# GeGLU feed-forward on one core: contraction chunks of neighbouring features, x transposed in two half rows and by transposing transfers

## The chip, the cores and the metric

The kernel runs on one core of a Trainium2 chip. The metric is device microseconds of one execution. Before the change the median of three runs is 299.9 us (299.17 to 300.43). The execution that was profiled took 299.69 us; its profile spans 298.4 us. TensorE's granted clock in the profile is 1.00.

## What is computed

```python
B, S, D, F = 32, 32, 1024, 3584            # x is (32, 32, 1024), all bf16
def reference(x, w_gate, w_up, w_down):
    return (_gelu(x @ w_gate) * (x @ w_up)) @ w_down    # _gelu: tanh approximation
```

With N = 32 x 32 = 1024 tokens: x is [1024, 1024], the gate and up weights are [1024, 3584], the down weights [3584, 1024], the output [1024, 1024]. The sum over D is cut into 8 chunks of 128 features (`dk`), F into 28 chunks of 128 rows of the hidden layer (`m`).

## The kernel before, in words

**Two large stages on TensorE.** In the first (L388) the weights are the stationary operand (128 features x 128 hidden rows), and transposed x (`xT`, features on the partitions, tokens along the free axis) moves. For each hidden chunk `m` and a block of tokens there are 8 gate matmuls and 8 up matmuls, which add up over `dk` in PSUM. ACT applies gelu to the gate sum (L446), DVE multiplies with the up sum and writes `hT` (L486). The second stage (L425) multiplies `hT` with the down weights; ACT and DVE by turns copy the sums out (L452, L492), and SP stores them (L344). A tuple of hidden chunk and token block is a *part*. Parts 0 to 7 are hidden chunks 0 to 7 with tokens 0 to 255; parts 8 to 15 the same hidden chunks with tokens 256 to 511; from part 16 on tokens come in blocks of 512.

**Which features are a chunk.** The program may choose which 128 of the 1024 features form a chunk, as long as weights and x agree. In the kernel before, partition p of chunk k holds feature 8p + k: `"(p k) f -> p k f"` for both weights (L211, L212). A chunk of x is then every eighth element of a row.

**How x gets transposed.** x lies in DRAM with tokens in rows; `xT` wants features on the partitions. Three ways are used:

- Tokens 0 to 255 are loaded into `xa` in two pieces of 128 tokens with whole rows of 2 KB: `xa` side 0 from SP, side 1 from ACT (L293). Chunks 0 to 4 are transposed on TensorE by a matmul with the identity (`turn_xa`, L349 to L360), ten matmuls into PSUM banks 3, 4 and 5 (`XA_PS`: bank 3 holds chunk 0, bank 4 chunks 1 and 2, bank 5 chunks 3 and 4). ACT copies each bank to `xT` (L439), three copies.
- Chunks 5 to 7 of those tokens are transposed by DVE in 32 x 32 blocks, sixteen instructions (L462).
- Tokens 256 to 1023 are loaded to `xs` in twelve pieces (`load_x`, L284, half from SP, half from ACT), laid out so that twenty DVE transposes (L477) fill `xT`. They are mixed by hand between the first products on DVE (`dve_order`, L186 to L194).

**Order of the work.** Every engine runs its instructions in program order, and waits are on semaphores. TensorE's order is the list `steps` (L156 to L183). It begins with seven warm-up matmuls of ones (L402), then the ten transposes, token side 0 before token side 1 (first chunks 0 to 2, then 3 and 4). Then come, with chunk 0, gate matmuls of parts 0, 1, 2, 3, 7, 6, 4, up matmuls of parts 0 to 3, the gate matmul of part 5, and up matmuls of 7, 6, 4, 5. A part whose PSUM bank was used by a transpose (3, 4, 5) has to wait for ACT's copy of that bank (L377 to L379). `together` then runs chunks 1 to 5 through all eight parts, and the parts are finished in two halves. Parts 8 to 11 follow with tokens 256 to 383 for chunks 0 to 3, tokens 384 to 511 for the same chunks, and the rest in 256 columns. All other parts go `one_by_one`.

**Queues.** SP issues its half of `xa`, then the weights of hidden chunks 0 to 7, one chunk `dk` at a time, gate and up in turn, 256 KB each (L289; the last chunk in two halves), then waits for up chunk 5 and issues its x pieces. After those have landed (`gate_w`, L308) SP loads the first small gate weight group and POOL the first small up group (L278). Later groups and the down weights wait for TensorE. ACT issues its half of `xa` and, after its three copies, its x pieces.

Of the kernel before, what the change touches and what calls it, by code (L numbers as in the profile page):

```python
# [5 lines left out]
P = 128  # L6
# [3 lines left out]
ALU = mybir.AluOpType  # L10
# [74 lines left out]
def bass_standalone__geglu_ffn__sampling_kernel(  # L85
# [40 lines left out]
    XC = N // 32  # L126
    XE = D // 4
    XA, XB, XC2 = (0, 256), (256, 512), (512, 1024)
    XB1, XB2 = (256, 384), (384, 512)
    XPIECES = [XB1, XB2, XC2]  # L130
# [5 lines left out]
    for t0, t1 in (XA, XB):  # L136
        for m in range(NBIG):
            parts.append((m, t0, t1, (m, 0, 256), (m, 256, 512)))
# [19 lines left out]
    def together(ps_, k0, k1, tok=None):  # L158
        for dk in range(k0, k1):
            for key in ("G", "U"):  # L160
                for p in ps_:
                    steps.append((p, key, dk, tok))

    def one_by_one(ps_, k0):
        for p in ps_:
            for key in ("G", "U"):
                for dk in range(k0, DK):
                    steps.append((p, key, dk, None))
# [12 lines left out]
    together(range(8, 12), 4, 6)  # L181
    one_by_one(range(8, 12), 6)
    one_by_one(range(12, NPART), 0)  # L183


    dve_order = []  # L186
    mix = ("E0 E1 E2 A0 E3 A1 A2 A3 B0 B1 B2 B3 E4 D4 D5 E5 D6 D7 E6 E7 "
           "C0 E8 C1 E9 C2 E10 E11 C3 C4 E12 C5 E13 C6 C7 E14 E15")
    for w in mix.split():
        if w[0] == "E":  # L190
            dve_order.append(("E", int(w[1:])))
        else:
            dve_order.append(("T", int(w[1:])) + {"A": XB1, "B": XB2, "C": XC2, "D": XB}[w[0]])
    dve_order += [("E", p) for p in range(NSHORT, NPART)]  # L194
# [15 lines left out]
    x_r = xf.rearrange("(c i) (a e) -> a i c e", i=32, a=4)  # L210
    wg_r = w_gate.rearrange("(p k) f -> p k f", k=DK)  # L211
    wu_r = w_up.rearrange("(p k) f -> p k f", k=DK)  # L212
# [7 lines left out]
    Q_X = {(q, s): _Clock(f"x{i}{s}", 16) for i, q in enumerate(XPIECES) for s in range(2)}  # L220
# [7 lines left out]
    all_clocks = [C_PE, C_ACT, C_DVE, C_POOL, *Q_XA, *Q_X.values(), *Q_W0.values(), *Q_W7.values(), *Q_WG, *Q_WU,  # L228
# [4 lines left out]
    with ExitStack() as es:  # L233
# [6 lines left out]
        assert 8 * N == XC * XE  # L240
        xs = hT[:, FM - 8:FM, :].rearrange("p a (b e) -> p (a b) e", e=XE)
# [39 lines left out]
        def load_x(ew, eng, q, side):  # L281
            c0, c1 = q[0] // 32, q[1] // 32
            for a in (2 * side, 2 * side + 1):
                v = ew.do(lambda: eng.dma_start(  # L284
                    xs[32 * a:32 * (a + 1), c0:c1, :], x_r[a, :, c0:c1, :]), clock=Q_X[(q, side)])
            ctx.set(("x", q, side), v)
# [5 lines left out]
        def early_loads(ew, eng, side):  # L292
            ctx.set(("xa", side), ew.do(lambda: eng.dma_start(  # L293
                xa[:, side, :], xa_r[:, side, :]), clock=Q_XA[side]))
            yield
            if side == 0:
                for k in range(DK - 1):
                    for w in ("wg", "wu"):
                        load_w0(ew, eng, w, k, 0, NBIG * P, Q_W0[(w, k)])
                for h in range(2):  # L300
                    for w in ("wg", "wu"):
                        load_w0(ew, eng, w, DK - 1, h * GSZ * P, (h + 1) * GSZ * P,
                                Q_W7[w] if h else Q_W0[(w, DK - 1)])
            ew.wait(Q_W0[("wu", 5)], ctx.get(("wu0", 5, 0)))
# [25 lines left out]
        def prog_sp(eng):  # L330
            sp = _Eng(ctx, eng, None)
            for _ in early_loads(sp, eng, 0):
                pass
# [13 lines left out]
            sp.wait(Q_OUT, last)  # L347

        def turn_xa(pe, eng, b, dk):  # L349
            pe.wait(Q_XA[b], ctx.get(("xa", b)))  # L350
            j = next(j for j, (_, k0, k1) in enumerate(XA_PS) if k0 <= dk < k1)
            bank, k0, k1 = XA_PS[j]
            o = 256 * (dk - k0) + P * b
            last = dk == k1 - 1 and b == 1
            v = pe.do(lambda: eng.matmul(  # L355
                ps[:, bank, o:o + P],
                xa[:, b, :].rearrange("p (j k) -> p j k", k=DK)[:, :, dk],
                ident[:, :], start=(dk == k0 and b == 0), stop=last), mark=last)
# [38 lines left out]
        WARM = [512] * 7  # L397
# [35 lines left out]
        def prog_act(eng):  # L433
            act = _Eng(ctx, eng, C_ACT)
            act.do(lambda: eng.activation(warm[:, 0:1], const0, ACTF.Gelu_apprx_tanh))
            for _ in early_loads(act, eng, 1):
                for j, (bank, k0, k1) in enumerate(XA_PS):
                    act.wait(C_PE, ctx.get(("XP", j)))
                    ctx.set(("XA", j), act.do(lambda: eng.activation(  # L439
                        xT[:, k0:k1, XA[0]:XA[1]],  # L440
                        ps[:, bank, 0:256 * (k1 - k0)].rearrange("p (k t) -> p k t", t=256), ACTF.Copy)))
# [13 lines left out]
        def prog_dve(eng):  # L455
            dve = _Eng(ctx, eng, C_DVE)

            for b in range(2):
                dve.wait(Q_XA[b], ctx.get(("xa", b)))
            for q in range(4):  # L460
                for a in range(4):
# [4 lines left out]
                            "p b (j k) -> p k b j", k=DK)[:, XA_DVE[0]:XA_DVE[1], :, 32 * a:32 * (a + 1)]))  # L466
            ctx.set("XD", v)
            for what in dve_order:
                if what[0] == "T":
                    dk, q = what[1], what[2:]  # L470
                    landed = [r for r in XPIECES if q[0] <= r[0] < q[1]]
                    for r in landed:
                        for s in range(2):
                            dve.wait(Q_X[(r, s)], ctx.get(("x", r, s)))
                    src = xs[:, q[0] // 32:q[1] // 32, :].rearrange(
                        "p c (j k) -> p c j k", k=DK)[:, :, :, dk]
                    v = dve.do(lambda: eng.transpose(  # L477
                        xT[:, dk, q[0]:q[1]].rearrange("p (c i) -> p c i", i=32), src))
                    for r in landed:
                        ctx.set(("T", dk, r), v)  # L480
                else:
                    i = what[1]
                    m, t0, t1, _gs, (ub, u0, u1) = parts[i]
                    dve.wait(C_ACT, ctx.get(("A", i)))
                    dve.wait(C_PE, ctx.get(("U", i)))
                    ctx.set(("D", i), dve.do(lambda: eng.tensor_tensor(  # L486
                        hT[:, m, t0:t1], t_bufs[i % NTB][:, 0:t1 - t0], ps[:, ub, u0:u1], ALU.mult)))
# [56 lines left out]
```

## Time and profile before

| what | us |
|---|---|
| median of the runs (3) | 299.9 (299.17 to 300.43) |
| the profiled execution | 299.69 |
| span of its profile | 298.4 |
| TensorE matmuls busy (PE) | 294.2 |
| DVE busy | 64.3 |
| ACT busy | 42.2 |
| first weights of stage one at TensorE | 5.18 |
| first matmul of parts 8 to 11 | 19.48 |
| first weights of the 512-column parts | 33.54 |
| start of stage two in the chain | 199.57 |

Times in the profile are microseconds from the start of its span. PE is TensorE's matmuls and PEld its weight loads, which run beside matmuls; SPq, ACTq and POOL lines with DMA in them are the issues of transfers. Each line of the timeline gives start, length, engine, line of the program, operation, output and inputs, the number of instructions merged into the line, and in brackets how long the engine was idle before it and what released it. Matmuls are pipelined, so a matmul's length is longer than the distance from one to the next; distances are read from the starts of the weight loads.

### The profile page before, as it was taken

To read this page: it belongs to the slowest core of one execution; us is meant where nothing else is said; L and a number is where in the kernel's file an instruction comes from. 1 tells how busy PE (TensorE), PEld (TensorE's weight loads), DVE (VectorE), ACT (ScalarE), POOL (GpSimd) and SP (SyncE) were. 2 spreads that over 40 slices of the span, in tenths; PEclk is the share of its full clock that TensorE was granted. 3 is DMA by queue.
4 is the path that set the end of the run, shared out by engine and by line. 5 is a ranking of instruction groups with operands and counts; after the bars stand their busy time and mean duration, and the time that the engine had idled before them with its cause. 6 is when DMAs were issued, how large, how long until landed. Compare 5 with 4: busy or idle time off the path is not lost.

```text
span 298.4 us, 3487 instructions
## 1 busy us (share of the span) xinstructions
PE 294.2 (99%) x1525; PEld 149.3 (50%) x1549; DVE 64.3 (22%) x108; ACT 42.2 (14%) x78; POOL 7.9 (3%) x14
## 2 busy tenths in 40 slices
PE   8999999999999999999999999999999999999997
PEld 5899644444444444444444444444444444444446
DVE  4669722111122111122111112110000000000000
ACT  3032211121111121111112111110000000000000
POOL 1001001020001002001000000000000000000000
PEclk9999999999999999999999999999999999999999
DMA  7997104856008301942104000000000100010001
GB/s 255 386 205 234 51 2 125 296 181 244 0 0 295 129 0 27 371 167 93 49 0 141 0 2 0 0 0 20 18 18 18 37 18 18 20 35 18 18 20 35
DMA packets 18094, 26.43 MB, mean 89 GB/s; under 512 B 1056, under 2 KB 11936, under 8 KB 18080
## 3 DMA queue, kind: packets, MB, share of 16 engines
q1 hardware_dynamic: 14128, 16.78, 17.3%
q0 software_dynamic: 2176, 8.39, 7.9%
q10 hardware_dynamic: 1776, 1.05, 1.4%
q8 instruction: 12, 0.20, 0.3%
q14 instruction: 2, 0.02, 0.0%
HBM read 24.12 MB, written 2.10 MB: 88 GB/s over the span
## 4 chain that ended last, share of the span: by engine, by line
PE 99%; issue 0%; ACT 0%
PE ps L388 65%; PE ps L425 32%; PE ps L402 1%; PE ps L355 0%; ACT xT L452 0%
## 5 line engine op out<-in xcount | busy, mean ns | idle before, releaser
L425 PE MATMUL ps<-wd,hT 128*128 128x512 bf16 (+1 forms) x468 | 96.5, 366 | 0.4
L388 PE MATMUL ps<-xT,wgbig 128*128 128x512 bf16 (+2 forms) x394 | 79.6, 337 | 0.3
L388 PE MATMUL ps<-xT,wubig 128*128 128x512 bf16 (+2 forms) x395 | 79.5, 336 | 0.3
L425 PEld LDWEIGHTS ps<-wd,hT 128*128 128x128 bf16 x476 | 46.6, 98 | 50.4
L486 DVE TENSOR_TENSOR hT<-tb,ps 128x512 bf16<-128x512 f32 (+1 forms) x64 | 38.9, 615 | 136.6 <-PE ps L388 136.6
L446 ACT ACTIVATE tb<-ps 128x512 f32<-128x512 f32 (+1 forms) x64 | 34.2, 544 | 158.3 <-PE ps L388 155.4
L388 PEld LDWEIGHTS ps<-xT,wgbig 128*128 128x128 bf16 x400 | 38.3, 98 | 31.7 <-DMA wgbig<-in_w_gate_dram 0.2
L388 PEld LDWEIGHTS ps<-xT,wubig 128*128 128x128 bf16 x400 | 38.1, 98 | 31.4
L388 PE MATMUL ps<-xT,wgsmall 128*128 128x512 bf16 x126 | 30.1, 379 | 0.1
L388 PE MATMUL ps<-xT,wusmall 128*128 128x512 bf16 x125 | 29.8, 379 | 0.2
L492 DVE CAST xT<-ps 128x512 bf16<-128x512 f32 (+1 forms) x8 | 5.3, 658 | 88.1 <-PE ps L425 88.1
L388 PEld LDWEIGHTS ps<-xT,wgsmall 128*128 128x128 bf16 x128 | 12.5, 98 | 15.1
L388 PEld LDWEIGHTS ps<-xT,wusmall 128*128 128x128 bf16 x128 | 12.5, 98 | 15.1
L452 ACT ACTIVATE xT<-ps 128x512 bf16<-128x512 f32 (+1 forms) x9 | 5.2, 573 | 93.1 <-PE ps L425 93.1
L477 DVE STREAM_TRANSPOSE xT<-hT 128x128 bf16<-128x128 bf16 (+2 forms) x20 | 13.4, 705 | 0.0
L462 DVE STREAM_TRANSPOSE xT<-hT 32x192 bf16<-32x192 bf16 x16 | 8.2, 514 | 4.7 <-DMA hT<-in_x_dram 4.2
L278 POOL DMA_DIRECT2D wubig<-in_w_up_dram x3 | 2.7, 884 | 62.9 <-PE ps L388 62.9
L402 PE MATMUL ps<-const-bfloat16-1.0 128*128 128x512 bf16 x7 | 3.1, 627 | 0.8 <-PEq L529 0.8
L278 POOL DMA_DIRECT2D wusmall<-in_w_up_dram x2 | 2.0, 993 | 47.9 <-PE ps L388 26.0
L272 POOL DMA_DIRECT2D wd<-in_w_down_dram x3 | 2.3, 766 | 19.1 <-PE ps L388 19.1
L402 PEld LDWEIGHTS ps<-const-bfloat16-1.0 128*128 128x128 bf16 x7 | 0.9, 139 | 2.1 <-issue 2.1
L439 ACT ACTIVATE xT<-ps 128x512 bf16<-128x512 f32 (+1 forms) x3 | 1.4, 527 | 2.4 <-PE ps L355 2.4
(10 smaller groups left out, 4.9 us busy)
## 6 DMA issues: line engine op xcount, KB each, us to landing
wd<-in_w_down_dram SPq DMA_DIRECT2D x4, 1024.0 KB, 11.3
wgbig<-in_w_gate_dram SPq DMA_DIRECT2D x3, 1024.0 KB, 5.8
wubig<-in_w_up_dram POOLq DMA_DIRECT2D x3, 1024.0 KB, 9.6
wd<-in_w_down_dram POOLq DMA_DIRECT2D x3, 1024.0 KB, 11.3
wgsmall<-in_w_gate_dram SPq DMA_DIRECT2D x2, 1024.0 KB, 5.9
wusmall<-in_w_up_dram POOLq DMA_DIRECT2D x2, 1024.0 KB, 9.7
out_dram<-xT SPq DMA_DIRECT2D x15, 128.0 KB, 1.7
wgbig<-in_w_gate_dram SPq DMA_DIRECT2D x7, 256.0 KB, 5.3
```

The lines of the kernel that those rows point to most:

```text
L272: ew.do(lambda: eng.dma_start(wd[:, a:b, :], wd_r[:, a:b, :]), clock=clock)
L278: ctx.set((w, j), ew.do(lambda: eng.dma_start(wbuf(w, buf)[:, :, 0:gsz * P], w_r[w][:, :, c0 * P:(c0 + gsz) * P]), clock=q))
L388: v = pe.do(lambda: eng.matmul(ps[:, bank, f0:f1], wbuf(w, buf)[:, dk, slot * P:(slot + 1) * P], xT[:, dk, t0:t1], start=first, stop=last ...
L402: pe.do(lambda: eng.matmul(ps[:, 0, 0:n], ones_w, ones_x[:, 0:n], start=True, stop=True), mark=False)
L425: v = pe.do(lambda: eng.matmul(ps[:, b, 0:ncols], hT[:, m, tc * P:(tc + 1) * P], wd[:, m, col0:col0 + ncols], start=(m == 0), stop=(m == F ...
L439: ctx.set(("XA", j), act.do(lambda: eng.activation(xT[:, k0:k1, XA[0]:XA[1]], ps[:, bank, 0:256 * (k1 - k0)].rearrange("p (k t) -> p k t", ...
L446: ctx.set(("A", i), act.do(lambda: eng.activation(t_bufs[i % NTB][:, 0:t1 - t0], ps[:, gb, g0:g1], ACTF.Gelu_apprx_tanh)))
L452: ctx.set(("E", ji), act.do(lambda: eng.activation(osb[:, tc, col0:col0 + ncols], ps[:, b, 0:ncols], ACTF.Copy)))
L462: v = dve.do(lambda: eng.transpose(xT[32 * a:32 * (a + 1), XA_DVE[0]:XA_DVE[1], XA[0]:XA[1]].rearrange("p k (b t) -> p k b t", t=P)[:, :, ...
L477: v = dve.do(lambda: eng.transpose(xT[:, dk, q[0]:q[1]].rearrange("p (c i) -> p c i", i=32), src))
L486: ctx.set(("D", i), dve.do(lambda: eng.tensor_tensor(hT[:, m, t0:t1], t_bufs[i % NTB][:, 0:t1 - t0], ps[:, ub, u0:u1], ALU.mult)))
L492: ctx.set(("E", ji), dve.do(lambda: eng.tensor_copy(osb[:, tc, col0:col0 + ncols], ps[:, b, 0:ncols])))
```

## The change

Chunk k now holds the neighbouring features 128k to 128k + 127, for weights and x. x's first 256 tokens are still loaded into `xa`, but in two halves of the row: piece 0 has features 0 to 511 of both token sides, piece 1 features 512 to 1023, in runs of 1 KB. Both are issued by SP, with the first gate weights between them. The matmul transposes read 128 neighbouring elements instead of every eighth; a transpose waits for the piece that has its chunk. Six of them (chunks 0 to 2, the two token sides in turn) come first, the four for chunks 3 and 4 only after the seven first gate matmuls. One warm-up matmul is left out. DVE's sixteen transposes for chunks 5 to 7 stay, read neighbouring elements and wait for piece 1 alone.

Tokens 256 to 1023 are no longer loaded to `xs` and transposed by DVE. SP issues six transposing transfers from x in DRAM straight into `xT`: two for tokens 256 to 511 (chunks 0 to 3 and 4 to 7), four for tokens 512 to 1023 (two chunks each), 256 KB each, after up chunk 6 has landed. TensorE waits for the transfer that brings a chunk, and parts 8 to 11 are no longer cut into two halves of tokens. `dve_order`, `load_x`, `x_r` and `xs` are gone, and with them ACT's issues of loads. The first small weight groups now wait for the last of the six transfers.

```diff
+    XTOK = {"B": (256, 512), "C": (512, 1024)}
+    XT = [("B", 0, 4), ("B", 4, 8), ("C", 0, 2), ("C", 2, 4), ("C", 4, 6), ("C", 6, 8)]
...
-    for k0, k1 in ((0, 3), (3, XA_DVE[0])):
-        for b in range(2):
-            steps += [("X", b, dk) for dk in range(k0, k1)]
-    for key, ps_ in (("G", (0, 1, 2, 3, 7, 6, 4)), ("U", (0, 1, 2, 3)), ("G", (5,)), ("U", (7, 6, 4, 5))):
-        steps += [(p, key, 0, None) for p in ps_]
+    steps += [("X", b, dk) for dk in range(0, 3) for b in range(2)]
+    steps += [(p, "G", 0) for p in (0, 1, 2, 3, 7, 6, 4)]
+    steps += [("X", b, dk) for dk in range(3, XA_DVE[0]) for b in range(2)]
+    steps += [(p, "U", 0) for p in (0, 1, 2, 3)] + [(5, "G", 0)] + [(p, "U", 0) for p in (7, 6, 4, 5)]
     together(range(0, 8), 1, 6)
...
-    together(range(8, 12), 0, 4, XB1)
-    together(range(8, 12), 0, 4, XB2)
-    together(range(8, 12), 4, 6)
-    one_by_one(range(8, 12), 6)
+    together(range(8, 12), 0, 4)
+    one_by_one(range(8, 12), 4)
...
-    wg_r = w_gate.rearrange("(p k) f -> p k f", k=DK)
-    wu_r = w_up.rearrange("(p k) f -> p k f", k=DK)
+    wg_r = w_gate.rearrange("(k p) f -> p k f", p=P)
+    wu_r = w_up.rearrange("(k p) f -> p k f", p=P)
...
+        def load_xa(ew, eng, h):
+            ctx.set(("xa", h), ew.do(lambda: eng.dma_start(
+                xa[:, :, 512 * h:512 * (h + 1)], xa_r[:, 0:2, 512 * h:512 * (h + 1)]), clock=Q_XA[h]))
+
+        def early_loads(ew, eng):
+            load_xa(ew, eng, 0)
+            for k in range(DK - 1):
+                for w in ("wg", "wu"):
+                    load_w0(ew, eng, w, k, 0, NBIG * P, Q_W0[(w, k)])
+                    if (w, k) == ("wg", 0):
+                        load_xa(ew, eng, 1)
...
+            ew.wait(Q_W0[("wu", 6)], ctx.get(("wu0", 6, 0)))
+            for q in XT:
+                (t0, t1), k0, k1 = XTOK[q[0]], q[1], q[2]
+                ctx.set(("xt", q), ew.do(lambda: eng.dma_start_transpose(
+                    xT[:, k0:k1, t0:t1], xf[t0:t1, k0 * P:k1 * P]), clock=Q_XT[q]))
...
-            pe.wait(Q_XA[b], ctx.get(("xa", b)))
+            pe.wait(Q_XA[dk // 4], ctx.get(("xa", dk // 4)))
...
-                xa[:, b, :].rearrange("p (j k) -> p j k", k=DK)[:, :, dk],
+                xa[:, b, dk * P:(dk + 1) * P],
...
-            for q in XPIECES:
-                if q[0] < t1 and t0 < q[1]:
-                    pe.wait(C_DVE, ctx.get(("T", dk, q)))
+            for q in XT:
+                if (t0, t1) == XTOK[q[0]] and q[1] <= dk < q[2]:
+                    pe.wait(Q_XT[q], ctx.get(("xt", q)))
...
-        WARM = [512] * 7
+        WARM = [512] * 6
...
-            for b in range(2):
-                dve.wait(Q_XA[b], ctx.get(("xa", b)))
+            dve.wait(Q_XA[1], ctx.get(("xa", 1)))
...
-                            "p b (j k) -> p k b j", k=DK)[:, XA_DVE[0]:XA_DVE[1], :, 32 * a:32 * (a + 1)]))
+                            "p b (k a i) -> p a k b i", a=4, i=32)[:, a, XA_DVE[0]:XA_DVE[1], :, :]))
```

More of the change, by code (lines that the diff above doesn't have):

```diff
@@ L120, in bass_standalone__geglu_ffn__sampling_kernel @@
     wd_gate_chunk = [min(FM - 1, 3 + 3 * k) for k in range(len(wd_groups))]
[L126 to L130, printed above, removed]
+    XA = (0, 256)
+    XTOK = {"B": (256, 512), "C": (512, 1024)}
+    XT = [("B", 0, 4), ("B", 4, 8), ("C", 0, 2), ("C", 2, 4), ("C", 4, 6), ("C", 6, 8)]
     XA_PS = [(3, 0, 1), (4, 1, 3), (5, 3, 5)]
@@ L135, in bass_standalone__geglu_ffn__sampling_kernel @@
     parts = []
-    for t0, t1 in (XA, XB):
+    for t0, t1 in (XA, XTOK["B"]):
         for m in range(NBIG):
@@ L156, in bass_standalone__geglu_ffn__sampling_kernel, with together @@
     steps = []
-    def together(ps_, k0, k1, tok=None):
+    def together(ps_, k0, k1):
         for dk in range(k0, k1):
@@ L161, in together @@
                 for p in ps_:
-                    steps.append((p, key, dk, tok))
+                    steps.append((p, key, dk))
     def one_by_one(ps_, k0):
@@ L167, in one_by_one @@
                 for dk in range(k0, DK):
-                    steps.append((p, key, dk, None))
-    for k0, k1 in ((0, 3), (3, XA_DVE[0])):
-        for b in range(2):
-            steps += [("X", b, dk) for dk in range(k0, k1)]
-    for key, ps_ in (("G", (0, 1, 2, 3, 7, 6, 4)), ("U", (0, 1, 2, 3)), ("G", (5,)), ("U", (7, 6, 4, 5))):
-        steps += [(p, key, 0, None) for p in ps_]
+                    steps.append((p, key, dk))
+    steps += [("X", b, dk) for dk in range(0, 3) for b in range(2)]
+    steps += [(p, "G", 0) for p in (0, 1, 2, 3, 7, 6, 4)]
+    steps += [("X", b, dk) for dk in range(3, XA_DVE[0]) for b in range(2)]
+    steps += [(p, "U", 0) for p in (0, 1, 2, 3)] + [(5, "G", 0)] + [(p, "U", 0) for p in (7, 6, 4, 5)]
     together(range(0, 8), 1, 6)
@@ L178, in bass_standalone__geglu_ffn__sampling_kernel @@
         one_by_one(half, 7)
-    together(range(8, 12), 0, 4, XB1)
-    together(range(8, 12), 0, 4, XB2)
-    together(range(8, 12), 4, 6)
-    one_by_one(range(8, 12), 6)
+    together(range(8, 12), 0, 4)
+    one_by_one(range(8, 12), 4)
     one_by_one(range(12, NPART), 0)
[L186 to L194, printed above, removed]
     jobs = []
@@ L209, in bass_standalone__geglu_ffn__sampling_kernel @@
     xa_r = xf.rearrange("(b p) d -> p b d", p=P)
-    x_r = xf.rearrange("(c i) (a e) -> a i c e", i=32, a=4)
-    wg_r = w_gate.rearrange("(p k) f -> p k f", k=DK)
-    wu_r = w_up.rearrange("(p k) f -> p k f", k=DK)
+    wg_r = w_gate.rearrange("(k p) f -> p k f", p=P)
+    wu_r = w_up.rearrange("(k p) f -> p k f", p=P)
     wd_r = w_down.rearrange("(m p) d -> p m d", p=P)
@@ L219, in bass_standalone__geglu_ffn__sampling_kernel @@
     Q_XA = [_Clock(f"xa{b}", 16) for b in range(2)]
-    Q_X = {(q, s): _Clock(f"x{i}{s}", 16) for i, q in enumerate(XPIECES) for s in range(2)}
+    Q_XT = {q: _Clock(f"xt{i}", 16) for i, q in enumerate(XT)}
     Q_W0 = {(w, k): _Clock(f"{w}0k{k}", 16) for k in range(DK) for w in ("wg", "wu")}
@@ L227, in bass_standalone__geglu_ffn__sampling_kernel @@
     Q_OUT = _Clock("out", 16)
-    all_clocks = [C_PE, C_ACT, C_DVE, C_POOL, *Q_XA, *Q_X.values(), *Q_W0.values(), *Q_W7.values(), *Q_WG, *Q_WU,
+    all_clocks = [C_PE, C_ACT, C_DVE, C_POOL, *Q_XA, *Q_XT.values(), *Q_W0.values(), *Q_W7.values(), *Q_WG, *Q_WU,
                   Q_WD_SP, Q_WD_POOL, Q_OUT]
@@ L239, in bass_standalone__geglu_ffn__sampling_kernel @@
         wd = sb("wd", [P, FM, D], BF16)
-        assert 8 * N == XC * XE
-        xs = hT[:, FM - 8:FM, :].rearrange("p a (b e) -> p (a b) e", e=XE)
         xa = hT[:, FM - 10:FM - 8, :]
@@ L279, in load_w @@
                 wbuf(w, buf)[:, :, 0:gsz * P], w_r[w][:, :, c0 * P:(c0 + gsz) * P]), clock=q))
[L281 to L286, printed above, removed]
         def load_w0(ew, eng, w, k, f0, f1, q):
@@ L290, in load_w0 @@
                 big[w][:, k, f0:f1], w_r[w][:, k, f0:f1]), clock=q))
[L292 to L304, printed above, removed]
-            for q in XPIECES:
-                load_x(ew, eng, q, side)
+        def load_xa(ew, eng, h):
[8 more added lines that the diff above has]
+                        load_xa(ew, eng, 1)
+            for h in range(2):
+                for w in ("wg", "wu"):
+                    load_w0(ew, eng, w, DK - 1, h * GSZ * P, (h + 1) * GSZ * P,
+                            Q_W7[w] if h else Q_W0[(w, DK - 1)])
+            ew.wait(Q_W0[("wu", 6)], ctx.get(("wu0", 6, 0)))
[3 more added lines that the diff above has]
+                    xT[:, k0:k1, t0:t1], xf[t0:t1, k0 * P:k1 * P]), clock=Q_XT[q]))
         def gate_w(ew, j):
             if war[j] is None:
-                for s in range(2):
-                    ew.wait(Q_X[(XC2, s)], ctx.get(("x", XC2, s)))
+                ew.wait(Q_XT[XT[-1]], ctx.get(("xt", XT[-1])))
                 return -1
@@ L331, in prog_sp @@
             sp = _Eng(ctx, eng, None)
-            for _ in early_loads(sp, eng, 0):
-                pass
+            early_loads(sp, eng)
             wd_mine = [k for k in range(len(wd_groups)) if k % 2 == 0]
@@ L360, in turn_xa, with part_step @@
                 ctx.set(("XP", j), v)
-        def part_step(pe, eng, opened, i, key, dk, tok):
+        def part_step(pe, eng, opened, i, key, dk):
             m, t0, t1, gs, us = parts[i]
             w, (bank, f0, f1) = ("wg", gs) if key == "G" else ("wu", us)
-            if tok is not None:
-                f0, f1 = f0 + tok[0] - t0, f0 + tok[1] - t0
-                t0, t1 = tok
             buf, slot, j = slot_of[m]
@@ L381, in part_step @@
                 pe.wait(C_DVE, ctx.get("XD"))
-            for q in XPIECES:
-                if q[0] < t1 and t0 < q[1]:
-                    pe.wait(C_DVE, ctx.get(("T", dk, q)))
+            for q in XT:
+                if (t0, t1) == XTOK[q[0]] and q[1] <= dk < q[2]:
+                    pe.wait(Q_XT[q], ctx.get(("xt", q)))
             first = (i, bank) not in opened
@@ L435, in prog_act @@
             act.do(lambda: eng.activation(warm[:, 0:1], const0, ACTF.Gelu_apprx_tanh))
[L436 to L441, printed above, removed]
+            for j, (bank, k0, k1) in enumerate(XA_PS):
+                act.wait(C_PE, ctx.get(("XP", j)))
+                ctx.set(("XA", j), act.do(lambda: eng.activation(
+                    xT[:, k0:k1, XA[0]:XA[1]],
+                    ps[:, bank, 0:256 * (k1 - k0)].rearrange("p (k t) -> p k t", t=256), ACTF.Copy)))
             for i, (m, t0, t1, (gb, g0, g1), us) in enumerate(parts):
@@ L465, in prog_dve @@
                         xa[32 * q:32 * (q + 1), :, :].rearrange(
-                            "p b (j k) -> p k b j", k=DK)[:, XA_DVE[0]:XA_DVE[1], :, 32 * a:32 * (a + 1)]))
+                            "p b (k a i) -> p a k b i", a=4, i=32)[:, a, XA_DVE[0]:XA_DVE[1], :, :]))
             ctx.set("XD", v)
[L468 to L487, printed above, removed]
+            for i, (m, t0, t1, _gs, (ub, u0, u1)) in enumerate(parts):
+                dve.wait(C_ACT, ctx.get(("A", i)))
+                dve.wait(C_PE, ctx.get(("U", i)))
+                ctx.set(("D", i), dve.do(lambda: eng.tensor_tensor(
+                    hT[:, m, t0:t1], t_bufs[i % NTB][:, 0:t1 - t0], ps[:, ub, u0:u1], ALU.mult)))
             for ji, (tc, col0, ncols, b) in enumerate(jobs):
```

## Prediction

> **What bounds the kernel now.** First the page: the span, the engine shares, the clock, the chain of what ended last.
>
> ```profile
> span 298.4 us, 3487 instructions
> PE 294.2 (99%) x1525; PEld 149.3 (50%) x1549; DVE 64.3 (22%) x108; ACT 42.2 (14%) x78; POOL 7.9 (3%) x14
> PEclk9999999999999999999999999999999999999999
> ...
> PE 99%; issue 0%; ACT 0%
> PE ps L388 65%; PE ps L425 32%; PE ps L402 1%; PE ps L355 0%; ACT xT L452 0%
> ```
>
> TensorE is the chain: 99% of it is matmuls, and DVE, ACT and the DMAs appear nowhere. In the chain in order of time the steady stretch repeats pieces of 10.74 + 0.05 us, that is 50 matmuls of 512 columns, 0.2158 us each. The change leaves those alone. It can move the time only where TensorE waits, where it runs slowly, or by making it wait. So I read the first 36 us as a timeline of TensorE's matmuls (PE) and weight loads (PEld) and of ACT.
>
> ```profile
> 0.77 3.15 PE L402 MATMUL ps<-const-bfloat16-1.0 128*128 128x512 bf16 x7 [0.77 <-PEq L529]
> 3.96 1.03 PEld L355 LDWEIGHTS ps<-ident,hT 128*128 128x128 bf16 x10 [0.96 <-issue]
> 4.65 1.36 ACT L439 ACTIVATE xT<-ps 128x256 bf16<-128x256 f32 x3 [2.43 <-PE ps L355]
> 5.18 1.08 PEld L388 LDWEIGHTS ps<-xT,wgbig 128*128 128x128 bf16 x7 [0.18 <-DMA wgbig<-in_w_gate_dram]
> 6.28 0.43 PEld L388 LDWEIGHTS ps<-xT,wubig 128*128 128x128 bf16 x4
> 6.71 0.10 PEld L388 LDWEIGHTS ps<-xT,wgbig 128*128 128x128 bf16 x1
> 6.82 0.42 PEld L388 LDWEIGHTS ps<-xT,wubig 128*128 128x128 bf16 x4
> 7.26 0.86 PEld L388 LDWEIGHTS ps<-xT,wgbig 128*128 128x128 bf16 x8
> ```
>
> Columns: start, length, engine, line. Seven warm-up matmuls, ten transposes of x by matmul, three copies of them by ACT, the first weights at 5.18, chunk 1 at 7.26; from there on no gap. The granted clock reads 1.00 throughout, but the pace tells more: warm-up weight loads are 0.425 us apart, the first 256-column ones after 5.18 about 0.21, those after 6.1 only 0.109. So **TensorE runs at half pace until about 6.1 us**.
>
> **The change, part by part.**
>
> *1. The front.* One warm-up matmul goes: the six end at 0.77 + 6 x 0.427 = 3.33 instead of 3.76. The transposes start when the first x piece lands. By the windows of one microsecond the DMAs had moved 0.31 MB by 3.0 and 0.67 MB by 4.0; the old pieces, 0.52 MB together, were complete near 3.6 and TensorE started at 3.96. The new first piece is 0.26 MB with nothing beside it, complete near 2.9. I take a start at 3.5 (bounds: 3.35, end of the warm-up; 4.0, as now).
>
> Six transposes come first, and the chunk 0 copy needs only two of them. ACT now starts 0.37 after the last transpose's weight load that it needs (4.28 to 4.65), takes 0.38, and the first weights follow 0.15 later. New: 3.5 + 0.105 + 0.37 + 0.38 + 0.15 = 4.5. The first gate weights are no obstacle: they are complete once 0.52 MB instead of 0.79 MB has moved (near 3.6 instead of 4.3; the load of up chunk 5, complete near 11.9, released SP at 12.71, a lag of 0.8), so about 4.4. The start is 0.7 earlier, but at half pace.
>
> Now the order bites. Seven gate matmuls at 0.213 end at 6.0. Only then come the four transposes of chunks 3 and 4, 0.25 at mixed pace: the last starts near 6.15. ACT's copy of them starts 0.3 later and takes 0.60 (its 512-column form), plus 0.15: part 5 may start at **7.2**. TensorE has only four up matmuls to put before it (0.44, to 6.7), then stands for 0.5 us, because it runs in order. Five matmuls follow (0.55), and chunk 1 starts at 7.74 where it now starts at 7.26: **+0.48**. In the kernel before that copy was done at 6.01, before part 5 at 6.71. Bounds: -0.02 if the copy is hidden after all (4.5 + 1.5 + 0.25 + 0.44 + 0.55 = 7.24), +0.9 if x starts at 4.0 as now.
>
> The second x piece now stands between the first weights on SP's queue; ACT's own issue (0.38) goes. Bytes up to the first up weights are unchanged (1.05 MB, near 5.1, landed 5.9), and they are wanted at 6.25. The next weight issues on SP are 0.47 later, but the DMAs are the limit there (318 to 408 GB/s; four issues in 1.9 us would be 550). Nothing for this. If it slips by 0.5 it disappears in the wait for part 5.
>
> *2. The DVE part of the first tokens (chunks 5 to 7).* Same sixteen transposes, now with neighbouring source elements. They took 8.69 us from 4.24. The second x piece lands near 5.1; at the old 0.51 each they end at 13.7, and chunk 5 is wanted at 7.74 + 4 x 1.745 = 14.7. Cover 1.0 us; at less than 0.51 each, more. If the cover is gone, what exceeds it is paid in full. Taken: nothing.
>
> *3. Weights by neighbouring rows.* Same number of 2 KB and 1 KB rows, at another pitch in DRAM. Early loads: chunk 1's weights are complete near 5.9, landed near 6.7, wanted at 7.74. Later groups are issued tens of microseconds ahead (a 1 MB load lands in 5.8 to 9.7). Taken: nothing; no row excludes a few per cent of rate either way, which this cover holds.
>
> *4. Tokens 256 to 511, no halves.* 64 matmuls of 128 columns ran from 19.48 to 23.11, that is 3.63. As 32 of 256 columns they take 32 x 0.109 = 3.49. **-0.14.**
>
> *5. DVE loses 20 transposes (13.4 us).* DVE was not in the chain; its products come earlier, and no matmul waited for one. The one wait shown for a DVE transpose, 0.17 of a weight load at 35.00, is hidden: matmuls go on at 0.216. Nothing.
>
> *6. The transposing transfers.* Six of 256 KB, on SP, after the last full up chunk but one. The 4.7 MB of early loads are unchanged, and chunk 6 completes 0.52 MB after chunk 5 at 366 to 383 GB/s: issue at 12.71 + 1.4 = 14.1. The trace has no such transfer. The nearest rows are the twelve x loads that they replace, as many bytes in runs of 512 B:
>
> ```profile
> L284 SPq DMA_DIRECT2D hT<-in_x_dram x6: 332/432/1630, 12.7 to 15.0; - x6
> L284 ACTq DMA_DIRECT2D hT<-in_x_dram x6: 368/453/1579, 12.7 to 15.0; - x6
> ...
> DMA to landing us min/median/max: 3.4/5.3/7.9
> ```
>
> Wanted: chunks 0 to 3 of tokens 256 to 511 at 19.48 + 0.48 = 19.96; chunks 4 to 7 at 23.45; tokens 512 up from 33.9 on, the last pair at 35.2. The first of the six, at the lowest to median landing, comes at 17.5 to 19.4: in time. All twelve old loads had landed by 22.9, 10.2 after issue: by that the six are in at 24.3, 11 us early. **Nothing**, if they overlap as the old ones did. Ends: no gain below nothing, since TensorE does not wait there now; at the longest landing, 7.9, the first comes at 22.0 and costs 2.0 (302.3); serial transfers are a rival below. Behind them on SP and POOL waits only the first small weight group (issued at 23.0 and 23.6 now), which is not wanted before 61, so 30 us of delay would be hidden.
>
> The Trainium skill ("DMA: Bandwidth & Descriptors", "Latency and other measured facts") gives 261 GB/s for a transposing transfer with a non-contiguous middle; by that, as an estimate, all six move in 6 us and the sum stays. The same skill ("VectorE: DVE Perf Modes", "The three transpose paths") gives 1309 ns for one 128x128 block by DMA; if blocks came one by one, an estimate of 10.5 us for each transfer and about 342 in all. No row here shows which holds.
>
> **Sum.** +0.48 - 0.14 = +0.34. The profiled execution took 299.69 (span 298.4 and 1.29 around it), 0.2 below the median 299.9. It becomes 300.03; against the median, 300.24: **300.2**. A difference under 0.5%, 1.5 us, is about what a measurement of this kernel cannot tell from no change.
>
> **Rivals.**
>
> *A, the wait in front is hidden.* Half pace ends before 6.0, or the last copy overlaps more. Chunk 1 at 7.24, sum -0.16: **299.7**. For it: only the order of one copy makes the 0.48. Against: the copy's 0.60 and the four matmuls' 0.44 are both rows.
>
> *B, half pace lasts longer.* Full pace came 5.3 us after the first matmul. The new front has holes: about 0.2 before the transposes, 0.3 before the first weights. If these restart the count at 4.5, full pace comes at 9.8. Up to chunk 1: 4.5 + 1.5 + 0.43, copy to 7.45, five matmuls at 0.213, so 8.5; then 1.3 us at half pace cost 0.65. Shift 1.9, less 0.14: **301.7**. For it: longer holes than now (0.2 and 0.15). Against: full pace came in spite of those. The Trainium skill ("TensorE: Matmul & The Clock Gate", "Part 1") says the clock is released after one busy window of some 3.4 us that runs freely; by it, as an estimate, a window missed costs 1.7.
>
> *C, slower: transposing transfers come one after another.* This is the case for the other side of no change. Place: the first matmuls of tokens 256 to 511 and of tokens 512 up. With t for each, the last pair lands at 14.1 + 6t and is wanted at 35.2: it decides from t = 3.5 on. At the median landing 5.3: the fourth chunk waits 1.25 (24.7 against 23.45), the last two pairs 4.6 and 4.9, together 10.7: **310.9**. At 7.9, 2.0 + 4.4 + 4.9 + 7.5 + 7.5 = 26.3: 326.5. For it: no row shows this kind of transfer. Against: 256 KB loads overlap on this queue (eighteen within 13 us), and 21 us of cover.
>
> *D, the change does not do what it says* (the first weights do not come earlier): within the bounds of part 1, 300.6.
>
> **Chances.** Forecast 0.60 with D in it, A 0.11, B 0.11, C 0.18 (of which up to 302.3: 0.03). Faster by over 0.5%: 0.02, a front much faster than A. Same: 0.70. Slower: 0.28, from B and C and a little of the forecast's edge. Range: forecast and A with the runs' scatter (299.2 to 300.4 around 299.9) start at 299.0; B and the late first transfer end at 302.4; outside is most of C.
>
> **What would show it.** Step 1: first gate weight load at 4.5, an idle gap of 0.5 before part 5's first gate matmul with ACT's last L439 copy as releaser, chunk 1 at 7.7. B: 256-column weight loads still 0.21 apart after 7. Step 4: 256-column matmuls 0.109 apart from 20.0. Step 6: landing under 3.5 us in effect, and no wait of PEld for xT from x in DRAM; such a wait would make the prediction wrong by its length. A span below 297 would contradict the reading that TensorE's own work bounds it.

## The result and the profile after

The changed kernel takes **300.27 us** (median of 22 runs, 299.68 to 301.99); the kernel before, measured beside it, 299.5 (22 runs, 299.17 to 300.43). The ratio is 1.0022, with a 95% interval of 1.0013 to 1.0031: slower by 0.2%, less than the 0.5% that the prediction set as its bound for "same". The forecast was 300.2. That the two agree so closely is partly luck: the prediction added +0.34 to a median of three runs (299.9) which 22 runs put at 299.5. The move was +0.77, more than twice the sum, and most of the difference lies in one term of step 1.

The page after, span, engines and chain:

```profile
span 299.1 us, 3414 instructions
PE 295.5 (99%) x1516; PEld 148.7 (50%) x1516; DVE 50.4 (17%) x88; ACT 42.4 (14%) x78; POOL 7.8 (3%) x14
...
PE 97%; DMA 2%; SPq 0%; ACT 0%; issue 0%
PE ps L362 65%; PE ps L399 32%; DMA wubig<-in_w_up_dram 2%; SPq L267 0%; SPq L263 0%; ACT xT L425 0%
```

A DMA is in the chain now, with 2% of the span: the load of up weights. Where it stands is told by the timeline of the front (L332 the transposes by matmul, L412 ACT's copies, L362 the gate and up matmuls):

```profile
3.72 0.56 PEld L332 LDWEIGHTS ps<-ident,hT 128*128 128x128 bf16 x6 [1.15 <-issue]
4.66 1.20 PEld L362 LDWEIGHTS ps<-xT,wgbig 128*128 128x128 bf16 x7 [0.38 <-DMA wgbig<-in_w_gate_dram]
5.92 0.58 PEld L332 LDWEIGHTS ps<-ident,hT 128*128 128x128 bf16 x4
6.80 0.60 ACT L412 ACTIVATE xT<-ps 128x512 bf16<-128x512 f32 x1 [1.61 <-PE ps L332]
7.17 0.33 PEld L362 LDWEIGHTS ps<-xT,wubig 128*128 128x128 bf16 x4 [0.67 <-DMA wubig<-in_w_up_dram]
7.17 0.61 PE L362 MATMUL ps<-xT,wubig 128*128 128x256 bf16 x4 [0.41 <-DMA wubig<-in_w_up_dram]
7.51 0.10 PEld L362 LDWEIGHTS ps<-xT,wgbig 128*128 128x128 bf16 x1
8.06 0.86 PEld L362 LDWEIGHTS ps<-xT,wgbig 128*128 128x128 bf16 x8
```

The first gate weights start at 4.66 instead of 5.18. But the first up weights land only at 7.13 by the chain, and TensorE waits for them until 7.17. ACT's copy of chunks 3 and 4 ends at 7.40; part 5, behind four up matmuls, loads at 7.51 without a further wait. So two ends nearly meet there. A third stands right behind them: by the landings that the trace records, the gate weights of chunk 1 landed at 8.00, 0.06 before they were used. Chunk 1 starts at 8.06 instead of 7.26. From there the two kernels are compared by distances between the same weight loads:

| stretch | before, us | after, us | difference |
|---|---|---|---|
| start of span to chunk 1 | 7.26 | 8.06 | +0.80 |
| chunk 1 to parts 8 to 11 | 12.22 | 12.23 | +0.01 |
| parts 8 to 15 | 14.06 | 13.97 | -0.09 |
| 512-column parts, to stage two | 166.03 | 166.03 | 0.00 |
| stage two to the end | 98.83 | 98.81 | -0.02 |

The sum, +0.7, is the difference of the spans (299.1 to 298.4). The transposing transfers cost nothing; the front is the whole loss.

Why are the up weights late? Windows of one microsecond, last column GB/s moved by the DMAs; first the kernel before, then the changed one:

```profile
4.00:5.00 1.00, 1.00 (x10) 1.00 (x10) 0.73 (x2) 0.35 (x2) 0.00 (x0) 1.00 1.12 354
5.00:6.00 1.00, 1.00 (x7) 0.57 (x5) 0.94 (x3) 1.00 (x3) 0.00 (x0) 1.00 0.92 318
```

```profile
4.00:5.00 1.00, 0.86 (x8) 0.56 (x6) 0.00 (x0) 0.80 (x2) 0.00 (x0) 1.00 1.18 269
5.00:6.00 1.00, 1.00 (x7) 0.69 (x6) 0.68 (x2) 0.19 (x1) 0.00 (x0) 1.00 0.84 250
```

By 6.0 us 1.13 MB have moved instead of 1.34. From 8 to 10 us the rates differ little (399 and 408 GB/s before, 391 and 401 after). The mean rate is only about half of the delay: the 1.05 MB up to the first up weights were reached near 5.7 instead of 5.1. The rest is in the last parts of the transfer. Each of these loads lands in sixteen parts, and the trace records the time of each. The parts of the first up weights landed between 5.20 and 5.82 in the kernel before and between 5.37 and 7.13 in the changed one, half of them by 6.06; TensorE needs all sixteen.

The transposing transfers of the changed kernel, the row that the prediction did not have:

```profile
L284 SPq DMA_TRANSPOSE xT<-in_x_dram x6: 1299/1302/1758, 15.4 to 22.6; - x6
...
DMA to landing us min/median/max: 3.2/3.7/4.1
```

SP spends 1.30 us on the issue of each (1.76 on the first, 0.43 on a plain load), so from the second on one starts about every 1.35 us, 194 GB/s of 256 KB pieces, and each lands about 3.7 after its issue.

### The profile page after: what moved, and what is told of

It reads as the page before. It is cut to its first block, busy times and chain, and to the rows that moved or that the text cites. A ratio compares the mean times of both kernels' runs of the same rounds, so it can differ in the third digit from the quotient of the medians.

```text
span 299.1 us, 3414 instructions
## 1 busy us (share of the span) xinstructions
PE 295.5 (99%) x1516; PEld 148.7 (50%) x1516; DVE 50.4 (17%) x88; ACT 42.4 (14%) x78; POOL 7.8 (3%) x14
## 4 chain that ended last, share of the span: by engine, by line
PE 97%; DMA 2%; SPq 0%; ACT 0%; issue 0%
PE ps L362 65%; PE ps L399 32%; DMA wubig<-in_w_up_dram 2%; SPq L267 0%; SPq L263 0%; ACT xT L425 0%
## 5 line engine op out<-in xcount | busy, mean ns | idle before, releaser
L362 PE MATMUL ps<-xT,wgbig 128*128 128x512 bf16 (+1 forms) x384 | 79.5, 346 | 0.1
L362 PE MATMUL ps<-xT,wubig 128*128 128x512 bf16 (+1 forms) x384 | 78.7, 344 | 0.4 <-DMA wubig<-in_w_up_dram 0.4
L362 PEld LDWEIGHTS ps<-xT,wgbig 128*128 128x128 bf16 x384 | 37.8, 99 | 32.1 <-DMA wgbig<-in_w_gate_dram 0.4
L362 PEld LDWEIGHTS ps<-xT,wubig 128*128 128x128 bf16 x384 | 37.5, 98 | 32.3 <-DMA wubig<-in_w_up_dram 0.7
L362 PE MATMUL ps<-xT,wusmall 128*128 128x512 bf16 x128 | 30.2, 379 | 0.0
L362 PE MATMUL ps<-xT,wgsmall 128*128 128x512 bf16 x128 | 30.2, 379 | 0.0
L362 PEld LDWEIGHTS ps<-xT,wusmall 128*128 128x128 bf16 x128 | 12.5, 98 | 15.1
L362 PEld LDWEIGHTS ps<-xT,wgsmall 128*128 128x128 bf16 x128 | 12.5, 98 | 15.1
L434 DVE STREAM_TRANSPOSE xT<-hT 32x192 bf16<-32x192 bf16 x16 | 5.9, 370 | 5.8 <-DMA hT<-in_x_dram 5.3
L412 ACT ACTIVATE xT<-ps 128x512 bf16<-128x512 f32 (+1 forms) x3 | 1.6, 526 | 3.6 <-PE ps L332 3.6
L332 PEld LDWEIGHTS ps<-ident,hT 128*128 128x128 bf16 x10 | 1.1, 141 | 1.3 <-issue 1.1
L332 PE MATMUL ps<-ident,hT 128*128 128x128 bf16 x10 | 1.4, 307 | 0.3 <-DMA hT<-in_x_dram 0.3
```

Of the source, the lines that this page charges most:

```text
L332: v = pe.do(lambda: eng.matmul(ps[:, bank, o:o + P], xa[:, b, dk * P:(dk + 1) * P], ident[:, :], start=(dk == k0 and b == 0), stop=last), ...
L362: v = pe.do(lambda: eng.matmul(ps[:, bank, f0:f1], wbuf(w, buf)[:, dk, slot * P:(slot + 1) * P], xT[:, dk, t0:t1], start=first, stop=last ...
L412: ctx.set(("XA", j), act.do(lambda: eng.activation(xT[:, k0:k1, XA[0]:XA[1]], ps[:, bank, 0:256 * (k1 - k0)].rearrange("p (k t) -> p k t", ...
L434: v = dve.do(lambda: eng.transpose(xT[32 * a:32 * (a + 1), XA_DVE[0]:XA_DVE[1], XA[0]:XA[1]].rearrange("p k (b t) -> p k b t", t=P)[:, :, ...
```

## The experiments

The theory after the result: two waits of nearly one length, for the first up weights and for ACT's copy of chunks 3 and 4, hold chunk 1; behind it nothing is lost. The rivals: one of the two alone; the rows of weights or the transposing transfers; the warm-up. The third wait, for the gate weights of chunk 1, was not in it. Medians are over 4 to 12 executions; each ratio is to the kernel before, run together with them. The last column is 260 for the changed kernel and 336 for the kernel before.

| run | median, us | ratio to before (95%) | early DMA rate, 4 to 6 us, GB/s |
|---|---|---|---|
| up weights before x's second piece | 300.95 | 1.0055 (1.0037 to 1.0074) | 241 |
| part 5 last | 300.35 | 1.0026 (1.0012 to 1.0040) | 218 |
| both | 300.13 | 1.0021 (1.0011 to 1.0030) | 306 |
| old front | 299.71 | 1.0005 (0.9994 to 1.0016) | 314 |
| x's second piece on ACT | 301.10 | 1.0036 (1.0019 to 1.0052) | 379 |
| the same, part 5 last | 301.32 | 1.0052 (1.0040 to 1.0064) | 365 |
| the same, all transposes first | 301.12 | 1.0044 (1.0028 to 1.0060) | 386 |
| whole rows, second side on SP | 302.27 | 1.0087 (1.0071 to 1.0103) | 286 |
| old front, six warm-ups | 299.65 | 0.9996 (0.9986 to 1.0007) | 361 |
| all transposes first, eight warm-ups | 299.74 | 1.0004 (0.9994 to 1.0014) | 320 |
| changed kernel, seven warm-ups | 300.47 | 1.0026 (1.0016 to 1.0036) | 247 |
| late transposing transfers | 301.52 | 1.0063 (1.0047 to 1.0078) | 235 |

**1. Up weights first.** In `early_loads`:

```diff
-                    if (w, k) == ("wg", 0):
+                    if (w, k) == ("wu", 0):
                         load_xa(ew, eng, 1)
```

> The changed kernel with one edit: the first up weights are issued before x's second half rows. In the changed kernel the first up matmul starts at 7.17, when these weights land, and chunk 1 at 8.06; ACT's copy of chunks 3 and 4 ends at 7.40. Theory 'two waits of one length' (copy and up weights each hold chunk 1 near 8.05): up matmuls start 0.5 to 0.8 earlier, then part 5 waits for the copy, chunk 1 at 8.0 to 8.1, time 300.3, no change. Theory 'up weights alone': chunk 1 at 7.4 to 7.6, time 299.7. Theory 'copy alone' (as in the prediction): no change, 300.3.

A miss in the time: it got slower. x's second piece, now third behind the weights, landed only at 7.0 and the transposes of chunk 4 waited for it; the copy then held part 5, as these lines say:

```profile
7.03 0.12 PEld L332 LDWEIGHTS ps<-ident,hT 128*128 128x128 bf16 x2 [0.85 <-DMA hT<-in_x_dram]
8.00 0.10 PEld L362 LDWEIGHTS ps<-xT,wgbig 128*128 128x128 bf16 x1 [0.53 <-ACT xT L412]
```

So TensorE can stand for this copy. But the copy was late here because x's piece was, not because of the order of steps that the prediction described, and the edit moved one load forward and another back. This run does not decide between the theories.

**2. Part 5 last.** In `steps`:

```diff
-    steps += [(p, "U", 0) for p in (0, 1, 2, 3)] + [(5, "G", 0)] + [(p, "U", 0) for p in (7, 6, 4, 5)]
+    steps += [(p, "U", 0) for p in (0, 1, 2, 3, 7, 6, 4)] + [(5, "G", 0), (5, "U", 0)]
```

> The changed kernel with one edit: both chunk 0 matmuls of part 5 come last, so that seven up matmuls (0.76 us) instead of four (0.44) stand between the late transposes and the one that needs ACT's copy. Theory 'two waits of one length': up matmuls still start at 7.17, nine matmuls of 0.109 follow, chunk 1 at 8.05 to 8.15, time 300.3, no change. Theory 'copy alone': chunk 1 at 7.6 to 7.7, time 299.8 to 299.9. Theory 'up weights alone': no change, 300.3.

No change, and the up matmuls start at 7.16, chunk 1 at 8.05. "Copy alone" falls. "Up weights alone" forecast the same as "two waits" and stays.

**3. Both edits.**

> The changed kernel with both edits: up weights before x's second half rows, and part 5 last. Theory 'two waits of one length': up matmuls start at 6.4 to 6.6, the copy (7.4) holds part 5 until 7.5, chunk 1 at 7.7, time 299.9 (0.35 less than the changed kernel). Theory 'up weights alone': the same as the first edit by itself. Theory 'copy alone': the same as the second edit by itself.

Chunk 1 at 7.70, as forecast by two waits. Part of that is not the edit: full pace came at about 5.2 in this execution, earlier than in the changed kernel's profile. The time, 300.13, is lower than the changed kernel's by less than the interval, so this run says little on its own; its lines show x's second piece late again (6.6) and a last wait of 0.20 for the copy.

**4. The old front.** `load_xa` and the order of transposes as before:

```diff
-                xa[:, :, 512 * h:512 * (h + 1)], xa_r[:, 0:2, 512 * h:512 * (h + 1)]), clock=Q_XA[h]))
+                xa[:, h, :], xa_r[:, h, :]), clock=Q_XA[h]))
...
+            load_xa(act, eng, 1)
...
-        WARM = [512] * 6
+        WARM = [512] * 7
```

> The changed kernel with the front of the kernel before: x's first tokens in two pieces of whole rows from SP and ACT, all ten transposes ahead of the first weights in the old order, seven warm-up matmuls. Rows of weights, transposing transfers and undivided parts 8 to 11 stay as changed. Theory 'the front is the whole loss': chunk 1 at 7.2 to 7.3 as before, parts 8 to 11 shorter by 0.09, time 299.4 against 299.5 of the kernel before. Rival 'transfers or rows cost something': it stays above 299.8, with a wait behind chunk 1 or slower early loads.

The median lies between the two forecasts, and the interval of its ratio includes 1, no change. The trace decides: chunk 1 starts at 6.96, parts 8 to 11 at 19.10, 512-column parts at 33.07, stage two at 199.10.

```profile
5.06 0.67 PEld L361 LDWEIGHTS ps<-xT,wgbig 128*128 128x128 bf16 x7 [0.37 <-DMA wgbig<-in_w_gate_dram]
5.89 0.33 PEld L361 LDWEIGHTS ps<-xT,wubig 128*128 128x128 bf16 x4 [0.16 <-DMA wubig<-in_w_up_dram]
6.96 0.77 PEld L361 LDWEIGHTS ps<-xT,wgbig 128*128 128x128 bf16 x8 [0.19 <-DMA wgbig<-in_w_gate_dram]
```

Behind chunk 1 all distances are those of the changed kernel or less (12.14, 13.97, 166.03). Rows of weights and transposing transfers are cleared; the up weights are there by 5.89. (Seven gate loads in 0.67 us: full pace had already come here. The profiled execution took 299.22, the low end of twelve times from 299.12 to 300.32.)

**5. x's second piece on ACT's queue.** Does its place on SP slow the early loads, or its short rows?

```diff
-                    if (w, k) == ("wg", 0):
-                        load_xa(ew, eng, 1)
...
+            load_xa(act, eng, 1)
```

> The changed kernel with one edit: x's second half rows are issued by ACT at the start, as the second piece was in the kernel before, and no longer by SP behind the first gate weights. In the changed kernel the DMAs move 250 to 270 GB/s between 4 and 6 us, in the kernel before 318 to 354. Theory 'the place on SP's queue slows the early loads': 300 GB/s or more between 4 and 6, first up weights landed at 5.8 to 6.0; then the copy of chunks 3 and 4 alone holds part 5 and chunk 1 starts at 7.5 to 8.0 (by the moment of full pace), time 299.9 to 300.2. Theory 'half rows are slow themselves': the slow stretch moves to 2 to 5 us, up weights still at 7, time 300.3 or more.

With the new place the slow stretch is gone, 391 and 367 GB/s between 4 and 6, and the up weights are waited for no more. Now the copy is the only wait, as the prediction had it:

```profile
6.99 0.68 PEld L360 LDWEIGHTS ps<-xT,wubig 128*128 128x128 bf16 x4
7.33 0.60 ACT L411 ACTIVATE xT<-ps 128x512 bf16<-128x512 f32 x1 [1.62 <-PE ps L330]
7.98 0.10 PEld L360 LDWEIGHTS ps<-xT,wgbig 128*128 128x128 bf16 x1 [0.31 <-ACT xT L411]
8.74 0.86 PEld L360 LDWEIGHTS ps<-xT,wgbig 128*128 128x128 bf16 x8
```

The time is a miss. x itself comes later (transposes at 4.24 instead of 3.72), and full pace late: the four up loads at 6.99 take 0.68 us, not 0.33. Its eleven times fall into two groups, five from 299.92 to 300.03, within the forecast, and six from 301.10 to 301.79. The profiled execution, 301.10, is of the upper group.

**6. The same with part 5 last.**

> As the run before, and both chunk 0 matmuls of part 5 last. Theory 'place on the queue, then the copy': seven up matmuls cover most of the copy, chunk 1 at 7.2 to 7.7, time 299.6 to 299.9. Theory 'half rows are slow themselves': up weights still at 7, nothing gained over the run before.

The wait for the copy is gone from the trace, but full pace came only near 9.2, after chunk 1 had started at 8.77, and the time is no better. What the edit is worth can't be read against that.

**7. All transposes first.**

```diff
-    steps += [("X", b, dk) for dk in range(0, 3) for b in range(2)]
+    steps += [("X", b, dk) for dk in range(0, XA_DVE[0]) for b in range(2)]
```

> The changed kernel with x's second half rows on ACT and all ten transposes ahead of the first gate weights, chunk by chunk. No copy is late then. Both theories of the copy: first gate weights at 4.9 to 5.0, part 5 without a wait, chunk 1 at 7.0 to 7.3, time 299.3 to 299.5, as the kernel before. If half rows are slow themselves: up weights at 7, chunk 1 at 8, time 300.2.

Gate weights at 5.26, no wait for copies or weights, and still chunk 1 at 8.44: gate and up loads are 0.21 apart until about 9.5.

**8. Whole rows, second side on SP.** The old front, with `load_xa(ew, eng, 1)` behind the first gate weights.

> The old front (whole rows by token side) in the changed kernel, but the second side of x issued by SP behind the first gate weights, where the change put its second half rows. Its transposes start late, since the first chunk needs both sides; what is read is the rate of the early loads. Theory 'place on SP's queue': 200 to 270 GB/s between 4 and 6 us, up weights near 7. Theory 'half rows are slow themselves': 310 GB/s or more between 4 and 6, up weights near 6. Time 300.0 to 300.8 by either.

207 GB/s between 4 and 5 and 365 in the microsecond after; the mean, 286, lies between the two forecasts. The second side lands at 6.1 and the up weights at 6.77, nearer to the first theory. Whole rows have a slow stretch there too, so the short rows are not needed for it. The time is a miss by either theory. The execution shows another thing, seen in the third column from the end, the granted clock:

```profile
7.00:8.00 1.00, 1.00 (x7) 0.79 (x8) 0.91 (x3) 0.81 (x2) 0.00 (x0) 0.71 1.02 361
8.00:9.00 1.00, 1.00 (x7) 0.73 (x5) 0.94 (x3) 0.00 (x0) 0.00 (x0) 0.50 1.02 385
9.00:10.00 1.00, 1.00 (x7) 0.69 (x6) 0.91 (x3) 0.00 (x0) 0.00 (x0) 0.50 1.04 402
```

After TensorE had stood for 2.0 us (to 6.17) the clock went to half for some 3 us. That is a part of the 302 only: of the four executions two have a mean granted clock of 0.994 (302.62, the profiled one, and 302.80), the other two 1.0 (301.71 and 301.92). The late start, gate weights at 6.94, is in all of them.

**9. Is it the warm-up?** Old front with `WARM = [512] * 6`, all transposes first with `WARM = [512] * 8`, and the changed kernel with `WARM = [512] * 7`.

> The changed kernel with the front of the kernel before, but six warm-up matmuls: they end at 3.33 and the transposes start near 3.95, a hole of 0.6 us instead of 0.2. Theory 'the hole decides when full pace comes' (seen in the three runs with x's second half on ACT, where the hole was 0.9 and full pace came at 7.4 to 9.9 in the profile): a part of the executions is longer by 1.2 to 1.8 us, median 300 to 301.2, full pace after 7 us in those. Rival 'the moment is chance alone': the same spread as with seven, median 299.5 to 299.8.

> x's second half rows on ACT, all ten transposes first, and eight warm-up matmuls, which end at 4.19, where x lands: no hole. Theory 'the hole decides': full pace by about 6, chunk 1 at 7.2 to 7.5, time 299.4 to 299.8, against 301.1 with six. Rival 'the moment is chance alone': 300.5 or more in half of the executions, as with six.

> The changed kernel with seven warm-up matmuls: they end at 3.76 instead of 3.33, and x lands at 3.7. Theory 'late up weights and copy make the loss': no change, transposes at 3.75 to 3.9, up matmuls still at 7.1, chunk 1 at 8.0 to 8.15, time 300.2 to 300.4. Rival 'the missing warm-up makes the loss': chunk 1 at 7.6 or earlier, time 299.8 or less.

The old front does as well with six (no time above 300.02 in 12, with a hole of 0.67 us at TensorE), so "the hole decides" is not borne out. It is not excluded either: by the same column the holes of experiments 5 to 7 are 0.79, 0.75 and 0.74, little longer, and full pace came at about 8.7, 9.2 and 9.5 there. With eight, all transposes first drops from 301.12 to 299.74, none of 11 above 300.03, and its chunk 1 starts at 7.44. The three slow ones ran on one chip and these on another, so chip and hole are not told apart there. The changed kernel gains nothing from a seventh warm-up:

```profile
6.29 0.60 ACT L412 ACTIVATE xT<-ps 128x512 bf16<-128x512 f32 x1 [1.11 <-PE ps L332]
7.21 0.33 PEld L362 LDWEIGHTS ps<-xT,wubig 128*128 128x128 bf16 x4 [1.13 <-DMA wubig<-in_w_up_dram]
8.10 0.86 PEld L362 LDWEIGHTS ps<-xT,wgbig 128*128 128x128 bf16 x8
```

The missing warm-up is not its loss. These lines also separate the two waits: full pace came at about 5.6, the copy was done at 6.89, and chunk 1 started no earlier. The late up weights are enough for the whole loss.

**10. Transposing transfers later.**

```diff
+            ew.wait(C_PE, ctx.get(("U", 0)))
             for q in XT:
```

> The changed kernel with the six transposing transfers held until TensorE has finished part 0 (18.2 us; now issued at 15.4 after up chunk 6). Theory 'the transfers are hidden, with about 1 us of cover for the first': the first lands at 21.9 to 22.3 and is wanted at 20.3, TensorE waits 1.6 to 2.0 there and nowhere else, time 301.9 to 302.3. Rival 'the first lands much earlier than the queue's last' (cover over 2.8 us): no wait, 300.3. Rival 'transfers come slower beside other work': further waits at the later chunks, over 303.

Issued at 18.21, the first landed at 21.46 and TensorE stood for it, once:

```profile
20.03 0.27 PE L363 MATMUL ps<-xT,wubig 128*128 128x256 bf16 x1
...
21.57 0.34 PEld L363 LDWEIGHTS ps<-xT,wgbig 128*128 128x128 bf16 x4 [1.33 <-DVE hT L444]
21.60 0.60 PE L363 MATMUL ps<-xT,wgbig 128*128 128x256 bf16 x4 [1.08 <-DMA xT<-in_x_dram]
```

(The view puts the weight load's idle time down to DVE; the chain of the run goes through the transfer, from 18.21 to 21.46.) By the changed kernel's distances part 8 would have started at 20.35: a stall of 1.2 and 1.25 in the median (300.27 to 301.52). The forecast of 1.6 to 2.0 took a landing of 3.7; this one took 3.25. No later chunk waits. In the changed kernel's profile the first transfer, issued at 15.42, landed at 18.64 by the recorded landings, which is 1.6 us of cover before 20.29.

The front of this execution is that of the changed kernel, and it shows the third wait. Full pace came at about 3.9, the up matmuls began at 6.66, and still chunk 1 was held, by its own gate weights:

```profile
8.12 0.77 PEld L363 LDWEIGHTS ps<-xT,wgbig 128*128 128x128 bf16 x8 [0.58 <-DMA wgbig<-in_w_gate_dram]
```

## Why the prediction was right, and where it was not

**The bound.** Right: from chunk 1 on the kernel is TensorE's own pace, 166.03 us in both.

**Step 1, the front: right sign, mis-sized.** The term was +0.48 and measured +0.80. The start came at 4.66 against 4.5, since x landed for 3.72 and not 3.5. Gate matmuls ended near 6.0, as worked out. The copy ended at 7.40 against 7.05. The sentence that failed is the one on the up weights: "Bytes up to the first up weights are unchanged (1.05 MB, near 5.1, landed 5.9) ... Nothing for this." The bytes were unchanged, the rate was not: 269 and 250 GB/s where the prediction carried over 354 and 318. They landed at 7.13, 1.2 late, about half of it by the rate and half because the last parts of the transfer came long after the first; the cover given for a slip, 0.5, was exceeded. The expected picture, an idle gap before part 5 with the copy as releaser, is not in the changed kernel's profile. It is in that of experiment 5, as described, and in those of experiments 1 and 3, where x's late piece made the copy late. Three ends of nearly one length stood there, the copy, the up weights and the gate weights of chunk 1, and the prediction saw the first. The third is in its step 3: "chunk 1's weights are complete near 5.9, landed near 6.7, wanted at 7.74"; the gate weights landed at 8.00.

**Step 2.** Right: DVE's sixteen took 0.37 each instead of 0.51, done before 11.7; nothing waits.

**Step 3.** Right on the rows, which cost nothing (experiment 4); but the cover that it gave the weights of chunk 1 was used up.

**Step 4.** -0.14 worked out, -0.09 measured: the 32 matmuls took 3.49 as forecast, but the stretch behind them 10.48 instead of 10.43. **Step 5.** Right, nothing: the distance from chunk 1 to parts 8 to 11 moved by 0.01.

**Step 6.** Right, nothing, but the times differ: issue at 15.42, not 14.1, as the early loads were late by as much; the last landed by about 26, wanted at 35.5. Of the two figures of the Trainium skill neither is what was measured: about 194 GB/s as SP issues them lies under the 261 of "DMA: Bandwidth & Descriptors", "Latency and other measured facts", and 1.35 us for 256 KB, eight blocks of 128x128, is far from 1309 ns a block ("VectorE: DVE Perf Modes", "The three transpose paths").

**Rivals.** A and D did not come. C falls: t is 1.35 us where it decides from 3.5. Experiment 10 shows what one late transfer costs when the cover is taken away, 1.25; no run had transfers as slow as the rival's. B is not the changed kernel's profile, in which full pace came near 6.1 as before. A late full pace was seen elsewhere at about the forecast price: the means of the two groups of experiment 5 lie 1.45 apart, and B was put 1.5 above the forecast (301.7 against 300.2). That a hole causes it is not shown. The Trainium skill ("TensorE: Matmul & The Clock Gate", "Part 1") holds that the window runs freely and that the moment varies by 500 ns either way. The trace agrees that it varies with the front unchanged, but by more: it came at about 3.9 in experiment 10 and near 6.1 in the changed kernel's profile. One of the 22 executions of the changed kernel, the slowest, 301.99, has a mean granted clock of 0.994 and all others 1.0; it was not profiled, and a clock that drops again, as in experiment 8, was in no rival.

**What stays open.** Why x's second piece on SP's queue slows the loads around it. With it on SP the seven profiles have 218 to 306 GB/s between 4 and 6 us, with it on ACT the seven have 314 to 386; but experiments 1 and 3, with the same loads, differ (241 and 306), so chance has a share. The landings part the two kinds more clearly: the fourth of the early transfers (1.05 MB in all) landed between 6.56 and 7.16 in the seven and between 5.73 and 6.46 in the others. No run tells the place from two things that went with it: on ACT the piece is issued at 0.78 instead of 1.65 to 2.21, and a second queue is in use. And why full pace came late in experiments 5 to 7 and not in 9. No version beat the kernel before: the best, the old front with the transposing transfers and six or seven warm-ups, cannot be told from it, nor can all transposes first with eight warm-ups.

## What to carry to other kernels

An earlier first matmul is worth nothing if the next operands keep their landing time: work out every arrival that the first microseconds need, and look for a second and a third end beside the one you found. A rate read from early loads belongs to their arrangement over queues; moving one load to another queue calls for bounds on that rate, not its reuse. Moving transposes from DVE to transfers cost nothing here, where TensorE is the bound and the transfers had cover, and gained nothing either, since DVE was not in the chain.

## What the runs showed of the hardware that was not expected

- SP needs 1.30 us to issue a transposing transfer of 256 KB, three times a plain one (0.43); in the changed kernel's profile it lands 3.2 to 4.1 us after the start of its issue.
- DVE's 32x192 block transposes take 370 ns from neighbouring elements and 512 ns from every eighth.
- The moment of full pace moves between executions and kernels from about 3.9 (experiment 10) to about 9.5 us (experiment 7) after the start of the span. The two groups of times of experiment 5, 1.1 to 1.9 us apart, fit that, though only one execution was profiled.
- In the profiled execution of experiment 8 the granted clock fell to 0.50 for about 3 us after TensorE had stood for 2.0 us. Its mean clock, 0.994, is also that of a second of the four executions, and of one each of the changed kernel (of 22), experiment 1 (of 6) and experiment 2 (of 12); all others have 1.0.
- A 256 KB load lands in sixteen parts that can drift apart: 0.6 us from first to last for the first up weights in the kernel before, 1.8 in the changed one.
